# One quarter of two weight units as narrow transfers, and every load list one quarter further

## The chip, the core and the metric

The kernel runs on one core of a Trainium2 chip: TensorE (PE, with PEld for its weight loads), VectorE (DVE), ScalarE (ACT), GpSimd (POOL), SyncE (SP), on-chip memory of 128 partitions, and 16 DMA engines that carry out the transfers which the engines issue into queues. The metric is the device time of one execution in microseconds. Before the change it is 435.75 us, the median of three runs (435.31 to 435.78).

## What is computed

Causal attention with a bias that only lowers scores, for 8 batches and 8 heads of 576 tokens by 64, then a mixing of the sequence in its spectrum: the first 64 modes of the real Fourier transform along the tokens are each multiplied by a complex 512 × 512 matrix of its own, transformed back, added to the attention output and passed through one more product with a ReLU:

```python
cum = np.cumsum(np.maximum(s, 0.0), axis=-1)
bias = -(cum[:, :, :, None] - cum[:, :, None, :])
scores = np.where(causal, -1e9, q @ kT / sqrt(64) + np.minimum(bias, 0.0))
x = (softmax(scores) @ v), heads side by side            # 8 x 576 x 512
X = np.fft.rfft(x, axis=1)                                # first 64 modes used
Yr = einsum('bmd,mde->bme', Xr, w_r) - einsum('bmd,mde->bme', Xi, w_i)
Yi = einsum('bmd,mde->bme', Xr, w_i) + einsum('bmd,mde->bme', Xi, w_r)
u = x + np.fft.irfft(Y, n=576, axis=1)
out = u + np.maximum(u @ w_ch, 0.0)
```

`w_r` and `w_i` are 64 × 512 × 512 in 4-byte floats, 67.1 MB each. Reading them is most of what the kernel moves.

## The kernel before

The attention goes in N = 32 steps n. A step is a group g of two heads (four groups) and one batch b: scores, softmax, product with v, and, one step behind, the Fourier transform of that batch's 128 channels (`fft`, `fft_pick`). When the eight batches of a group are through, its part of the mode products can be taken: the matrices of the modes, 128 rows of them for each group. Those of groups 0 to 2 are done inside the later steps (`mode_products`, sums in `y_acc`), those of group 3 after the last step (`modes`, matmuls at L605 and L628), followed by the inverse transform and the product with `w_ch`.

The weights pass through five tiles `w_sb`, and at first through space in `x_all` and `y_acc` that is not yet in use. For groups 0 to 2 they are cut into 24 units u (group u // 8, sixteen modes c = u % 8 // 2, `w_r` or `w_i` by u % 2). A unit takes four loads, called quarters (`unit_loads`, L249): quarter h goes to the 32 partitions from 32h on, four modes j with 2048 values each (4 rows of 512), 512 KB as 2-byte floats in the tile, 1 MB as 4-byte floats in memory; the transfer converts. Group 3's come as 16 tiles of two loads (64 partitions each; the last is cut finer), `tile_loads` at L270.

All loads of weights, q, k and v are issued by POOL into one queue, q0, in the order in which the program gives them. Before each step a list of them is made (L727): the q and k of a coming step (`loads_qk`), its v, and as many quarters as are wanted on the chip by then, `loads_w(on_chip[n])`. `load` (L311) deals the lists evenly into one another:

```python
todo = [((i + 0.5) / len(l), x) for l in lists for i, x in enumerate(l)]
for _, (dst, src) in sorted(todo, key=lambda t: t[0]):
    nc.gpsimd.dma_start(out=dst, in_=src)
```

`on_chip[n]` counts quarters; `fits` (L326) lowers the count where a tile's former unit has not been used yet by step n. A POOL load waits for the load eight before it, and where it overwrites something for the engine that last read it: a q or k load (tile `qk`) for the transposes on PE (`tr_ps`, L454), a weight load for the mode products (`yp`, L605). `loads_w` is called again after the last step and inside `modes` (L645) for the rest of group 3.

SP has its own queue, q1. For each step from 2 on it loads the two rows of the running sums into one partition of `qt` (`cum_rows`, L441, 1 × 2 × 576 values), waiting for PE's transposes. At the end of the weights it issues `mark` (L1040), a tiny copy out of the very last weights loaded, so it waits for that load; behind it in SP's order stand the copies `yv` (L662) that spread a result over partitions, and later the outputs (L977, L981, L984).

Of the kernel before, what the change touches and what calls it, by code (L numbers as in the profile page):

```python
# [19 lines left out]
def kernel(  # L20
# [12 lines left out]
    B, H, S, D = q.shape  # L33
    NM = moe_w_r.shape[0]
    DM = H * D
    P = 128
# [189 lines left out]
    HU = WM * DM  # L226

    def slot(i, x, n=1):

        return w_sb[i][:, x * WM : (x + n) * WM, :].rearrange("p m e -> p (m e)")  # L230
# [8 lines left out]
    def parts_of(u):  # L239

        if u == 0:
            return [(0, xg[:, : 4 * HU])]
        if u == 1:
            return [(0, ya[:, HU:]), (3, xg[:, 4 * HU : 5 * HU])]
        return [(0, slot(UNIT_AT[u], 0, 4))]

    wt = {}

    def unit_loads(u):  # L249

        g, c, ri = u // NCK, u % NCK // 2, u % 2
        src = (moe_w_r, moe_w_i)[ri][:, g * P : (g + 1) * P, :]
        slots, todo = [], []
        for j0, t in parts_of(u):
            slots += [t[:, i : i + HU].rearrange("p (q e) -> p q e", q=QD) for i in range(0, t.shape[1], HU)]
        for h in range(QD):
            todo.append([])
            for j0, t in parts_of(u):
                first = 1 if ri == 1 and c + h + j0 == 0 else 0
                j1 = j0 + t.shape[1] // HU  # L260
                todo[-1].append((
                    t[QP * h : QP * h + QP, first * HU :].rearrange("p (j x) -> p j x", x=HU),
                    src[16 * c + 4 * (j0 + first) + h : 16 * c + 4 * j1 - 3 + h : 4].rearrange(
                        "j (p q) e -> p j (q e)", q=QD
                    ),
                ))
        wt[g, c, ri] = slots
        return todo

    def tile_loads(k):  # L270

        c, ri = divmod(k, 2)
        src = (moe_w_r, moe_w_i)[ri][:, (NG - 1) * P :, :]
        i, x = TILE_AT[k]
        t = slot(i, 2 * x, 2).rearrange("p (m e) -> p m e", e=DM)
        m0 = 2 * MC * (c // 2) + 2 * (c % 2)
        todo = []
        for x0, x1 in [(0, 4)] if k < NT3 - 1 else [(0, 2), (2, 4)]:
            for h in range(2):
                first = 1 if ri == 1 and c == 0 and x0 + h == 0 else 0  # L280
                todo.append((
                    t[HP * h : HP * h + HP, 2 * (x0 + first) : 2 * x1].rearrange("p (m q) e -> p m (q e)", q=2),
                    src[m0 + 4 * (x0 + first) + h : m0 + 4 * x1 - 3 + h : 4].rearrange(
                        "m (p q) e -> p m (q e)", q=2
                    ),
                ))
        wt[NG - 1, c, ri] = [t[:, :WM], t[:, WM:]]
        n = len(todo) // 2
        return [todo[:n], todo[n:]]

    NLW = 4 * NUN + 2 * NT3
    asked, queued = [0], []

    def loads_w(upto):
        todo = []
        while asked[0] < min(upto, NLW):
            if not queued:
                t = asked[0]
                queued.extend(unit_loads(t // 4) if t < 4 * NUN else tile_loads((t - 4 * NUN) // 2))
            todo += queued.pop(0)  # L300
            asked[0] += 1
        return todo

    def place_of(t):
# [21 lines left out]
    def fits(w, done):  # L326

        holds = {}
        for t in range(min(w, NLW)):
            item, end = (t // 4, t // 4 * 2 + 1) if t < 4 * NUN else (t // 2, t // 2)  # L330
            for x in place_of(t):
                if x in holds and holds[x][0] != item and holds[x][1] >= done:
                    return t
                holds[x] = item, end
        return min(w, NLW)

    on_chip = []
    for n in range(N):
        if n < B:
            w = 4 + (4 * NU + 2) * (n + 1) // (B + 1)  # L340
        else:
            w = 3 * n + 2 if n < 2 * B + 4 else max(59, 4 * n - 22)
        on_chip.append(fits(w, used[n]))


# [3 lines left out]
    first = loads_qk(0)  # L349
    load(first[:2])  # L350
    load(loads_w(2 * W0), loads_v(0) + loads_tails(0) + first[2:] + loads_v(1))
    nc.sync.dma_start(out=Ff_sb.rearrange("p T c -> p (T c)"), in_=d_Ff)
    nc.sync.dma_start(out=G_sb[:, :S], in_=d_G)
# [11 lines left out]
    with tc.tile_pool(name="cum_psum", bufs=1, space=PSUM) as cpsum:  # L365
# [29 lines left out]
        for x in range(2):  # L395
            rows = slice(NL * x, NL * x + NL)
# [222 lines left out]
    def modes(g, c, meanwhile=None, ris=(0, 1)):  # L619
# [16 lines left out]
        for x in range(2 * ris[0], 2 * ris[-1] + 2):  # L636
# [3 lines left out]
            for z in range(4):  # L640
                if meanwhile:
                    product(ri, z // 2, 2 * y + z % 2)
                else:
                    product(ri, y, z)
        load(loads_w(fits(NLW, 2 * NUN + 2 * c + ris[-1] + 1)))  # L645
        if ris[-1] == 0:
            nc.vector.tensor_tensor(out=y_acc[:, c, :], in0=ps, in1=y_acc[:, c, :], op=ALU.add)
# [68 lines left out]
    with tc.tile_pool(name="sc_psum", bufs=2, space=PSUM) as scpool, \  # L716
# [8 lines left out]
        for n in range(N):  # L725
            tails_due = loads_tails(n // B + 1)[n % B - 3 : n % B - 2] if 2 < n % B < 5 else []
            load((loads_qk(n + LA) if n % 2 else []) + (loads_vs(n) if n else loads_v(LA)) + tails_due, loads_w(on_chip[n]))  # L727
            if n == N - B:
                nc.gpsimd.dma_start(out=wch_sb, in_=moe_w_ch.rearrange("(dt p) e -> p dt e", p=P))
# [18 lines left out]
            i = first_pairs[n - N + len(first_pairs)] if n >= N - len(first_pairs) else None  # L748
# [350 lines left out]
    for step in (  # L1099
# [8 lines left out]
        i = int(step[1:].rstrip("ab"))  # L1108
# [34 lines left out]
```

## Time and profile before

The profiled execution took 435.96 us, of which the span that the profile shows is 434.2 us (mean granted TensorE clock 0.972).

| | before |
|---|---|
| median of three runs | 435.75 us |
| profiled execution / its span | 435.96 / 434.2 us |
| busy: PE, DVE, ACT, POOL | 380.6, 256.5, 249.5, 136.5 us |
| read from memory / written | 163.29 / 9.51 MB, 398 GB/s over the span |
| packets in POOL's queue q0 | 40400, 81.28 MB (as written on the chip) |
| weight loads of 512 KB: issue to landing | 17.5 us (`w_r`, 60 of them), 16.9 us (`w_i`, 55) |
| `qk` loads of 288 KB: issue to landing | 13.8 and 14.7 us (15 each) |

The page gives busy time by engine, then the span in 40 slices with the busy share in tenths for each engine and for the DMA engines, with GB/s. A group's line has what an instruction writes and reads, its count, its mean, and the idle time ahead of it with what ended that. The waits list, for each engine and line, what it waited for: total us, times, longest. The chain of work that ended last is cut short in this page at the last instructions and tells nothing of the weights, so the waits and the timeline are read in its place.

### The profile page before, as it was taken

What the parts mean: (1) busy time and instruction counts of PE and PEld (TensorE: products, weight loads), DVE (VectorE), ACT (ScalarE), POOL (GpSimd) and SP (SyncE); (2) the same over time, 40 slices, a digit from 0 to 9 for tenths busy, and PEclk for the clock granted to TensorE, in tenths of its full rate; (3) what the DMA queues carried; (4) which work ended last, traced back from release to release, by engine and by line L of the source; (5) the groups of instructions that cost most, each with busy time, mean ns of one, the idle gap of its engine ahead of it and who ended that gap; (6) DMA issues with size and microseconds to landing.
All of it is one profiled execution on the core that took longest, in us unless ns stands there. A gap on an engine that the chain in (4) does not pass through costs nothing. (4 is left out here: it accounts for less than half of the span.)

```text
span 434.2 us, 12629 instructions
## 1 busy us (share of the span) xinstructions
PE 380.6 (88%) x5395; PEld 220.2 (51%) x5395; DVE 256.5 (59%) x574; ACT 249.5 (57%) x556; POOL 136.5 (31%) x218
## 2 busy tenths in 40 slices
PE   1599999999999999999998898979879777877994
PEld 1256666546666655665665455545544334533441
DVE  7555656526775756667665565554636443671795
ACT  1387777717767765666775356545542343451894
POOL 6463333131333223233322222222222222210582
PEclk9999999989999999999999699998989998999998
DMA  8999999999999999999999999999999999995798
GB/s 157 210 207 210 214 207 209 213 214 210 210 211 211 207 212 214 212 211 208 211 212 212 212 212 211 213 212 214 212 210 212 211 211 211 211 211 103 224 365 316
DMA packets 47105, 92.87 MB, mean 214 GB/s; under 512 B 8222, under 2 KB 17946, under 8 KB 47050
## 3 DMA queue, kind: packets, MB, share of 16 engines
q0 software_dynamic: 40400, 81.28, 99.5%
q1 hardware_dynamic: 6650, 10.80, 7.4%
q8 instruction: 42, 0.69, 0.6%
q14 instruction: 13, 0.11, 0.1%
HBM read 163.29 MB, written 9.51 MB: 398 GB/s over the span
## 5 line engine op out<-in xcount | busy, mean ns | idle before, releaser
L513 ACT ACTIVATE p_sb<-sc_ps,cumt_sb 128x320 f16<-128x320 f32 (+1 forms) x384 | 161.1, 519 | 37.6 <-PE sc_ps L504 37.6
L504 PE MATMUL sc_ps<-qt,kt 128*64 128x256 bf16 (+3 forms) x640 | 95.9, 295 | 2.3 <-ACT kt L458 1.7
L504 PEld LDWEIGHTS <-kt 128*128 128x128 bf16 (+1 forms) x640 | 50.5, 126 | 62.7 <-issue 36.0
L315 POOL DMA_DIRECT2D w_sb<-in_moe_w_i_dram x62 | 35.2, 568 | 88.0 <-DMA w_sb<-in_moe_w_r_dram 32.0
L458 DVE COPY qt<-tr_ps 64x576 bf16<-64x576 bf16 x64 | 47.7, 745 | 18.3 <-PE tr_ps L454 18.0
L550 DVE RECIPROCAL rcp<-av_ps 128x5 f32<-128x5 f32 x64 | 12.4, 194 | 77.9 <-PE av_ps L545 77.9
L315 POOL DMA_DIRECT2D w_sb<-in_moe_w_r_dram x60 | 34.0, 567 | 77.5 <-DMA w_sb<-in_moe_w_r_dram 24.3
L493 PE MATMUL sc_ps<-negm,ident 128*128 128x512 bf16 x128 | 51.0, 399 | 0.0
L545 PEld LDWEIGHTS <-p_sb 128*128 128x128 f16 x1088 | 40.7, 98 | 3.6
L454 PE MATMUL tr_ps<-ident,qk 64*64 64x64 bf16 x1152 | 31.6, 198 | 10.7 <-DVE kt L458 5.2
L475 ACT ACTIVATE p<-sc_ps,cumt 128x64 f16<-128x64 f32 x32 | 10.1, 314 | 53.3 <-PE sc_ps L471 53.3
L458 ACT COPY kt<-tr_ps 64x576 bf16<-64x576 bf16 x32 | 22.9, 716 | 23.7 <-DVE qt L458 23.2
L454 PEld LDWEIGHTS <-qk 64*64 64x64 bf16 x1152 | 24.3, 112 | 23.2 <-DVE kt L458 8.3
L496 PE MATMUL sc_ps<-negm,ident 128*128 128x256 bf16 x128 | 35.9, 281 | 0.0
L545 PE MATMUL av_ps<-va,p_sb 128*128 128x65 f16 x768 | 35.0, 194 | 0.0
L605 PE MATMUL yp<-w_sb,xs 64*32 64x512 bf16 (+1 forms) x704 | 30.9, 414 | 4.3 <-DMA w_sb<-in_moe_w_i_dram 2.3
L551 DVE TENSOR_TENSOR x_all<-av_ps,rcp 128x320 f16<-128x320 f32 x64 | 31.5, 492 | 2.2
L617 DVE TENSOR_TENSOR y_acc<-yp,y_acc 128x512 f32<-128x512 f32 x34 | 21.9, 687 | 14.9 <-PE yp L605 14.9
L545 PE MATMUL av_ps<-vb,p_sb 128*128 128x65 f16 x320 | 26.0, 195 | 0.0
L315 POOL DMA_DIRECT2D vr<-in_v_dram x22 | 15.1, 687 | 31.1 <-DMA w_sb<-in_moe_w_r_dram 8.8
L458 DVE COPY kt<-tr_ps 64x576 bf16<-64x576 bf16 x32 | 24.4, 763 | 0.4
L684 ACT COPY w_sb<-z_ps 128x512 f32<-128x512 f32 x20 | 11.7, 587 | 22.5 <-PE z_ps L703 16.1
(127 smaller groups left out, 539.3 us busy)
## 6 DMA issues: line engine op xcount, KB each, us to landing
w_sb<-in_moe_w_r_dram POOLq DMA_DIRECT2D x60, 512.0 KB, 17.5
w_sb<-in_moe_w_i_dram POOLq DMA_DIRECT2D x55, 512.0 KB, 16.9
out_dram<-w_sb SPq DMA_DIRECT2D x16, 512.0 KB
qk<-in_q_dram POOLq DMA_DIRECT2D x15, 288.0 KB, 13.8
qk<-in_k_dram POOLq DMA_DIRECT2D x15, 288.0 KB, 14.7
vr<-in_v_dram POOLq DMA_DIRECT2D x14, 256.0 KB, 15.5
x_all<-in_moe_w_r_dram POOLq DMA_DIRECT2D x4, 512.0 KB, 9.9
y_acc<-in_moe_w_i_dram POOLq DMA_DIRECT2D x3, 384.0 KB, 7.1
```

Of the source, the lines that this page charges most:

```text
L315: nc.gpsimd.dma_start(out=dst, in_=src)
L454: nc.tensor.transpose(ps[rows, r, :], src[rows, r, :], ident16[rows, rows])
L458: copy(out=to[:, :, :, half * RH : half * RH + RH], in_=ps[HP * i : HP * i + HP].rearrange("d r (h p) -> d h p r", h=2),)
L493: nc.tensor.matmul(ps[:, : 2 * W], ident16, both, start=True, stop=False, skip_group_check=True)
L496: nc.tensor.matmul(ps[:, S : S + W], ident16, negm[:, NMB + m0 : NMB + m0 + W], start=True, stop=False, skip_group_check=True,)
L504: nc.tensor.matmul(ps[rows, c0 : c0 + i1 - i0], keys, qh[:, i0:i1], start=False, stop=True, skip_group_check=True,)
L513: nc.scalar.activation(out=pt[:, o : o + n_], in_=ps[:, c0 : c0 + n_], func=ACTF.Exp, bias=cumt_sb[:, x, pidx : pidx + 1], scale=0.125,)
L545: nc.tensor.matmul(ps[:, I, :NCH], lhsT, rhs, start=(i == 0), stop=(i == len(todo) - 1), skip_group_check=True,)
L550: nc.vector.reciprocal(out=rcp, in_=ps[:, :, D])
L551: nc.vector.tensor_tensor(out=x_all[:, g, b, :, D * h : D * h + D], in0=ps[:, :, :D], in1=rcp.unsqueeze(2).to_broadcast([P, NT, D]), op=AL ...
L605: nc.tensor.matmul(ps[hp][32 * j : 32 * j + 32, :], cols[k0:k1, q_, c0 : c0 + 4 * B, 4 * c + j], wt[g, c, ri][j][k0:k1, q_, :], start=(ri ...
L617: nc.vector.tensor_tensor(out=y, in0=ps[hp], in1=y, op=ALU.add)
```

## The change

There are two edits. In units 7 and 12, quarter 1 (partitions 32 to 63) no longer goes as one transfer. Its place in the order keeps a transfer of 16 partitions (32 to 47). The other 16 partitions follow as four transfers of eight partitions: partitions 48 to 55 whole (8 × 4 × 2048 values); then of partitions 56 to 63 the first 128 values of modes 0 and 1 (8 × 2 × 128), the other 1920 values of all four modes (8 × 4 × 1920), and the first 128 values of modes 2 and 3. Each is put into the list when the count of quarters asked for has reached 4u + 2 plus the number in `BEHIND`, so that other quarters lie between, and, as the lists are dealt into one another, q, k and v loads too. POOL issues 207 loads in place of 199; the bytes are the same.

The second edit raises `on_chip` by one quarter (512 KB on the chip, 1 MB read) from step 8 on. `fits` lowers the raised count only at step 31, to 102, which is the count before the change too.

```diff
+    BEHIND = {7: (1, 3, 5, 9), 12: (1, 3, 5, 7)}
+    pieces = []
     wt = {}
 
     def unit_loads(u):
...
         wt[g, c, ri] = slots
+        if u in BEHIND:
+            (dst, src), = todo[1]
+            todo[1] = [(dst[:16], src[:16])]
+            for i, after in enumerate(BEHIND[u]):
+                rows = slice(24, 32) if i else slice(16, 24)
+                x = slice(0, HU) if i == 0 else slice(P, HU) if i == 2 else slice(0, P)
+                j = (slice(0, 4), slice(0, 2), slice(0, 4), slice(2, 4))[i]
+                pieces.append((4 * u + 2 + after, (dst[rows, j, x], src[rows, j, x])))
         return todo
...
             todo += queued.pop(0)
             asked[0] += 1
+            while pieces and pieces[0][0] == asked[0]:
+                todo.append(pieces.pop(0)[1])
         return todo
...
         if n < B:
             w = 4 + (4 * NU + 2) * (n + 1) // (B + 1)
         else:
-            w = 3 * n + 2 if n < 2 * B + 4 else max(59, 4 * n - 22)
+            w = 3 * n + 3 if n < 2 * B + 4 else max(60, 4 * n - 21)
         on_chip.append(fits(w, used[n]))
```

The order of POOL's loads round unit 7 (numbers are partitions) is then: the 32 partitions of its quarter 0; a v load; the 16 partitions; quarter 2; eight partitions whole; a v load; quarter 3; the first quarter of unit 8; the first tiny piece; a quarter; q; a quarter; k; the piece of 8 × 4 × 1920; v; three quarters with a v load among them; the second tiny piece; the next q and k.

## Prediction

> **What bounds the kernel now.** I read four views: the page's slices and queues, the waits, the timeline round the last load, and windows by stage.
>
> The page (40 slices of 10.9 us; queues with packets, MB and share of sixteen DMA engines' time):
>
> ```profile
> DMA  8999999999999999999999999999999999995798
> GB/s 157 210 207 210 214 207 209 213 214 210 210 211 211 207 212 214 212 211 208 211 212 212 212 212 211 213 212 214 212 210 212 211 211 211 211 211 103 224 365 316
> ...
> q0 software_dynamic: 40400, 81.28, 99.5%
> ...
> q8 instruction: 42, 0.69, 0.6%
> q14 instruction: 13, 0.11, 0.1%
> ```
>
> The transfers run at one rate, some 211 GB/s, until slice 36. q0 holds POOL's loads, four fifths of which are weights. Two small queues, q8 and q14, fetch instructions on the same engines; they matter below.
>
> The waits (what waits for what: us in total, times, longest), POOL's, then SP's, then PE's:
>
> ```profile
> POOL w_sb L315 <- DMA w_sb<-in_moe_w_r_dram: 56.4, 32, 2.5
> POOL w_sb L315 <- DMA w_sb<-in_moe_w_i_dram: 42.9, 24, 2.6
> POOL qk L315 <- PE tr_ps L454: 27.3, 7, 7.9
> ...
> SPq L1040 <- DMA w_sb<-in_moe_w_i_dram: 64.1, 1, 64.1
> ...
> PE tr_ps L454 <- DMA qk<-in_k_dram: 3.4, 2, 2.1
> ```
>
> POOL issues a load when the eighth before it has landed, so about eight are under way and POOL waits for the transfers, not they for it. Its longest other wait is 7.9 us for PE.
>
> The timeline at the last weight load (start, length):
>
> ```profile
> 399.21 0.65 PE L628 MATMUL yp<-w_sb,xs 128*32 128x512 bf16 x4 [0.41 <-DMA w_sb<-in_moe_w_i_dram]
> 399.22 0.26 SPq L1040 DMA_DIRECT2D mark<-w_sb  x1
> 399.53 0.63 SPq L662 DMA_DIRECT2D yv<-y_sb  x1
> ```
>
> The last load lands at 399.17 us; 35.0 us of tail follow to the end at 434.2. Loads of the tail (no weights) don't change, so the time moves one for one with that landing. 434.2 + 1.8 us around it make the profiled run's 435.96, 0.2 above the median 435.75; I subtract from both alike.
>
> Windows by stage (us; PE, PEld, DVE, ACT, POOL busy; clock; DMA share; GB/s):
>
> ```profile
> 36.00:228.00 192.00, 187.53 (x3195) 115.29 (x3194) 121.67 (x292) 130.89 (x309) 57.43 (x97) 0.99 1.12 211
> ...
> 312.00:396.00 84.00, 67.75 (x688) 36.59 (x688) 39.81 (x69) 31.75 (x60) 18.24 (x30) 0.96 1.10 207
> ```
>
> PE is 98% busy early, but idle 16.2 us in the 84 before the end: what delays PE early is made up there, unless it delays POOL's loads.
>
> **The sixteen engines don't end together.** The trace has each engine's completion of each load. For the last weight load they spread over 391.80 to 399.17 us. Behind the last one stand, in us: 0, 0.45, 1.27, 1.43, 1.44, 1.46, 1.80, 1.90, then 2.57, then 4.21, 5.03, 5.86, 6.00, 6.64, 6.87, 7.36. At 18 us the spread was 1.4 us. Two things drive it apart. Each 16 KB packet of q8 holds one engine 0.95 us and makes the next three packets slower, 1.1 us in all; 42 packets over eight engines are 5 or 6 each, 5.6 to 6.7 us: these are the eight latest ("the fetching eight"). The packet durations show the fetches coming round with period eight. The two-row loads of `qt` (30 of them, L441) put a 1152-byte packet and a completion on two engines, some 0.06 us each, 1.8 us in all; followed through the completions, these two belong to the other eight. One of them, called b here, also took about four half-microsecond steps that coincide with q14's 8 KB packets (13 in all) and is the ninth late one, 2.57 us behind the last.
>
> **The change part by part.** *Narrow transfers.* From the packet records an engine starts its next packet after 305 ns for 4096 bytes, 154 for 2048, 79 for 1024, 41 for 512: 0.074 ns per byte, so 286 for 3840 bytes and 22 for 256. A completion adds 8 ns. A whole quarter is 8 packets of 4096 bytes on each engine: 8 × 305 + 8 = 2.45 us. In its place: the 16-partition transfer, 4 packets on each of sixteen, 1.23 us; eight rows of 4 × 4096, on eight engines 1.23 us; eight rows of 4 × 3840, 1.15; two tiny ones, 2 × 22 + 8 = 0.05 each. Neither "eight engines" nor which eight is shown in this trace. Few-row loads here do stay on few engines (two for `qt`). If successive narrow transfers take turns between two groups of eight, the order big, tiny, big, tiny puts both big ones on the same eight:
>
> loaded eight: 1.23 + 1.23 + 1.15 + 0.02 = 3.63 instead of 2.45: +1.18 a unit, +2.36 for two (0.02 for completions posted by all);
> relieved eight: 1.23 + 0.05 + 0.05 + 0.02 = 1.35 instead of 2.45: −1.10, −2.20 for two.
>
> *Which eight.* Few-row transfers begin at some first engines; `qt`'s two lie outside the fetching eight. That is the only row that bears on it, and I take it: the first group of eight is the one without fetches, and the fetching eight are relieved. New lateness against today's last: fetching eight 0 − 2.20; b −2.57 + 2.36 = −0.21; the next −4.21 + 2.36 = −1.85. Engine b is the new last: **−0.2 us**. Nine tenths of the fetching eight's gain are lost to one engine. Bounds: −2.2 if b is spared, +2.36 if the loaded eight are the fetching ones.
>
> [...]
>
> *Port price of few partitions.* No load into 8 partitions is in the trace. Nearest rows: the `yv` spreads into 16 partitions, 128 packets of 1024 bytes in 0.71 to 0.76 us, 172 to 185 GB/s against the stream's 215 (16 × 4096 bytes in 305 ns), and slower ones (1.2 to 1.7 us) beside outputs. Bounds: 0 and a factor 215/182 = 1.18 on the 7.2 us that the loaded engines spend in narrow ones, +1.3 us. Between these I take 0: b trails the next of the loaded engines by 0.9 to 1.2 us (at 110 us 2.5 against 1.3; at 180 us at least 2.8 against 1.9), so it works on its narrow piece, 1.2 us long, when its neighbours have nearly left theirs. [...]
>
> *Eight more issues on POOL* (207 instead of 199), 0.56 us each: 4.5 us, hidden in its 56.4 + 42.9 us of waits for weights. What would remove the cover is an engine running dry. From the completions, at every issue after 20 us even the fastest engine has at least 3.4 us queued; eight under way now include tiny ones, and replaying the stream with the new sizes leaves at least 3.3 us. If it were gone, each dry spell would cost up to an issue, 0.6 us.
>
> *One quarter more from step 8 on.* Bytes and their number stay; the order changes: `qk` and `vr` loads stand behind one more quarter, at most 2.45 us later. What is late next is PE's transposes (L454). Spare of `qk` tiles before use: 1.2 to 1.5 us at steps 18 and 22, 5.9 at 24, none at 26 and 30 (the 3.4 us above). So PE may lose up to 2.45 us at some four steps; 10 at the most, against the 16.2 idle. POOL waits for tr_ps too (the 27.3 us), and with it every load behind; the slowest of these left 4.8 us of queued transfers, 2.35 after a 2.45 us delay. SP's `qt` loads (L441) wait on the same transposes, and no weight waits for SP. I take 0; bounds 0 and +2.45 (one such cover gone wholly). Nothing here makes the landing earlier: engines never stop, so asking earlier buys nothing.
>
> Sum: −0.2 + 0 + 0 + 0 = −0.2 us; 435.75 − 0.2 is 435.55, given as **435.5**.
>
> **Rivals.** (A measurement here can tell about 0.2%, 0.87 us.)
>
> 1. *The loaded eight are the fetching eight* (the other side): +2.36 on the last engine, **438.1**. For: nothing shows which group begins. Against: `qt`'s engines. It decides as soon as the latest fetching engine gets more than 0.87 us extra. A mixed group (narrow transfers not beginning at a boundary) gives +0.5 to +2.4.
>
> 2. *b is spared.* The half-microsecond q14 steps of b need not fall on b again once the program differs: 13 packets over eight engines are 1.6 each, b has four. With the mean b ends 1.2 us earlier, new last −1.4: **434.3**; at best −2.2, the fetching eight: 433.5. Decides from 0.7 us less on b. For: only four events make b late. Against: the same loop issues the same instructions, so they may well fall alike.
>
> 3. *Narrow pieces are slowed* by their few partitions: −0.2 + 1.3 = **436.9**, more if neighbours run abreast. For: 172 to 185 against 215 GB/s. Against: b's distance.
>
> 4. *PE late, then POOL late*: **436.8 to 438.2** (+1 to +2.45). For: `qk` with no spare at two steps. Against: 16.2 us idle, 2.35 us cover.
>
> 5. *The eight-row transfers spread over all sixteen*: no shift, four more completions a unit cost 8 × 8 ns = 0.06 us: **435.8**. The change would not do what it is shaped for.
>
> **How the numbers follow.** Likeliest 0.38 (own range 434.9 to 436.4: −0.8 for b's q14 steps, +0.9 for ports or PE in part); rival 1 0.17; rival 2 0.27; rival 3 0.08; rival 4 0.06; rival 5 0.04. Faster: rival 2, 0.27. Same: likeliest and rival 5, 0.42. Slower: 1, 3 and 4, 0.31. The range reaches into rival 2 as far as −1.65 (434.1) and past rival 1's 438.1 to 438.3; left out are the best of rival 2 (0.1) and the worst of 3 and 4 and a mixed sum (0.1).
>
> **What the changed kernel's profile will show.** Right: the eight-row pieces' data packets on eight engines; the spread of the last weight load's completions shrinks from 7.4 to about 5 us, with one engine last and the fetching eight 2 us behind it; L1040's issue stands 35.0 us before the end, at 399.0. Rival 1: the spread grows to about 12 us and L1040 to 401.6. Rival 2: L1040 at 397 to 398, b among the rest. Rival 3: packets of the narrow pieces longer than 305 ns. Rival 4: longer waits of PE for `qk` and of POOL for tr_ps, and idle transfers in the slices. Rival 5: sixteen engines with data for each piece. q8 still has about 42 packets. The prediction is wrong above all if lateness isn't additive engine by engine, or if other small queues fall elsewhere.

## The result and the profile after

The changed kernel takes 440.38 us, the median of six runs (439.08 to 443.13), against 436.01 us for the kernel before in the same comparison: 1.0109 times as long by the comparison of the runs, 95% interval 1.0081 to 1.0137 (the medians alone give 1.0100). Ratios and intervals below are of the same kind, each against the kernel before in its own comparison. The forecast was 435.5 us with a range up to 438.3. The profiled execution has a span of 438.9 us, 4.7 more than before.

The slices and queues of the changed kernel's page (40 slices, now of 11.0 us each):

```profile
DMA  8999999999999999999999999999999999996598
GB/s 160 208 209 210 212 210 207 214 214 211 208 210 209 209 213 207 191 205 201 156 209 214 213 210 212 212 212 213 215 211 211 212 212 210 211 212 126 196 366 324
...
q0 software_dynamic: 40784, 81.28, 99.2%
...
q8 instruction: 42, 0.69, 0.6%
q14 instruction: 13, 0.11, 0.1%
```

Bytes and instruction fetches are those of before; of the 384 packets more, 64 have 256 bytes (the tiny pieces) and 320 have 4 bytes; eight more loads with sixteen completions each make 128 of these, and what the other 192 are for the records do not show. The rate is what changed: 191, 205, 201 and 156 GB/s in the slices from 175 to 219 us, where before no slice from the second to the 36th lay under 207. That is where unit 12 is loaded.

Windows by stage, the same stretches in both kernels (PE, PEld, DVE, ACT, POOL busy; clock; DMA share; GB/s). Before:

```profile
100.00:122.00 22.00, 21.81 (x364) 13.37 (x362) 15.77 (x38) 15.46 (x37) 6.75 (x12) 1.00 1.12 211
170.00:186.00 16.00, 15.85 (x294) 9.85 (x294) 10.80 (x26) 11.91 (x28) 4.86 (x9) 1.00 1.10 211
206.00:212.00 6.00, 5.92 (x114) 3.96 (x113) 3.81 (x12) 4.99 (x12) 2.16 (x4) 1.00 1.13 208
```

After:

```profile
100.00:122.00 22.00, 21.81 (x373) 13.67 (x372) 14.89 (x36) 16.33 (x39) 6.98 (x12) 1.00 1.12 209
170.00:186.00 16.00, 15.85 (x273) 9.47 (x273) 11.41 (x26) 9.39 (x22) 4.38 (x8) 1.00 1.14 193
206.00:212.00 6.00, 6.00 (x82) 3.05 (x79) 4.16 (x11) 3.41 (x8) 1.31 (x3) 0.68 0.77 121
```

Where unit 7 is loaded (100 to 122 us) little is lost, 209 GB/s against 211. Round unit 12 two different things happen. From 170 to 186 us the DMA engines are busier than before (1.14 against 1.10) and move less (193 against 211): their packets take longer. What the 4096-byte packets that start there last beyond 324 ns, the median, adds up to 22.2 us against 0.4 before. From 206 to 212 they are partly idle (0.77 against 1.13). Why the same pieces cost so much less round unit 7 was not found.

The waits of PE between 80 and 230 us explain the second:

```profile
PE yp L617 <- DMA w_sb<-in_moe_w_r_dram: 6.7, 2, 6.3
PE yp L617 <- DMA w_sb<-in_moe_w_i_dram: 2.3, 2, 1.9
```

Before, PE had no wait for weights in that time. L617 is the mode product (L605 before). The timeline of PE, and then of POOL:

```profile
203.66 1.93 PE L617 MATMUL yp<-w_sb,xs 64*32 64x512 bf16 x28 [6.27 <-DMA w_sb<-in_moe_w_r_dram]
```

```profile
210.69 0.59 POOL L327 DMA_DIRECT2D qk<-in_q_dram  x1 [6.40 <-PE tr_ps L466]
```

By the completion records the last tiny piece of unit 12 landed at 203.62 us. It had been put behind the 57th quarter, which step 18 asks for, and step 20 multiplies with unit 12. PE stood 6.3 us, its granted clock was 0.50 from 200 to 206 us, and POOL's next q load waited 6.4 us for PE's transposes; with eight loads under way at 203.59 us and nothing new until 210.69, when the last three of them were still landing, engines ran dry: 121 GB/s from 206 to 212 us against 208 before. At step 14 the last piece of unit 7 came 1.9 us late in the same way (141.15 us, PE at 141.19). By the start times of the steps' normalisation on DVE, step 21 stood 12.3 us later than before, step 31 only 1.9.

The end, as shown for before: the last weight load lands at 402.56 us, 3.4 later than before.

```profile
402.61 0.26 SPq L1052 DMA_DIRECT2D mark<-w_sb  x1
402.93 0.62 SPq L674 DMA_DIRECT2D yv<-y_sb  x1
```

PE's product with these weights:

```profile
404.45 0.65 PE L640 MATMUL yp<-w_sb,xs 128*32 128x512 bf16 x4
```

From there to the end it is 36.3 us in place of 35.0. PE starts it only at 404.45, 1.9 us after the landing and with no idle time ahead of it, where before it followed the landing by 0.04 us. So 3.4 of the 4.7 us are transfers and 1.3 are PE behind.

The sixteen completions of that load now stand, behind the last, between 0 and 3.44 us, against 7.36 before. The narrower spread isn't the gain that was forecast: in the dry spell at 206 to 212 us the early engines had nothing to do until new loads came, the earliest from 207.14 us on. That this is what closed the spread was not tried.

### The profile page after: what moved, and what is told of

It is laid out like the page before. It is cut to its first block, busy times and chain, and to the rows that moved or that the text cites. A ratio compares the mean times of both kernels' runs of the same rounds, so it can differ in the third digit from the quotient of the medians.

```text
span 438.9 us, 12639 instructions
## 1 busy us (share of the span) xinstructions
PE 381.5 (87%) x5395; PEld 220.5 (50%) x5395; DVE 256.6 (58%) x574; ACT 248.9 (57%) x556; POOL 140.6 (32%) x226
## 5 line engine op out<-in xcount | busy, mean ns | idle before, releaser
L327 POOL DMA_DIRECT2D w_sb<-in_moe_w_i_dram x66 | 37.5, 569 | 91.4 <-DMA w_sb<-in_moe_w_r_dram 29.6
L327 POOL DMA_DIRECT2D w_sb<-in_moe_w_r_dram x64 | 36.1, 564 | 86.5 <-DMA w_sb<-in_moe_w_r_dram 31.5
L617 PE MATMUL yp<-w_sb,xs 64*32 64x512 bf16 (+1 forms) x704 | 31.1, 409 | 10.9 <-DMA w_sb<-in_moe_w_r_dram 6.7
L617 PEld LDWEIGHTS <-xs 64*32 64x32 bf16 (+1 forms) x768 | 16.4, 139 | 21.4 <-issue 16.3
```

What stands on the lines that cost most here:

```text
L617: nc.tensor.matmul(ps[hp][32 * j : 32 * j + 32, :], cols[k0:k1, q_, c0 : c0 + 4 * B, 4 * c + j], wt[g, c, ri][j][k0:k1, q_, :], start=(ri ...
```

## The experiments

Two theories were set against each other at first, and a third came from the first results. **L**: the last pieces are late for PE. **E**: eight engines carry more, among them late ones. **N**: packets that go into few neighbouring partitions get in each other's way. N came out of the packet records: the 4096-byte packets that start between 90 and 230 us last 324 ns in the median, and what they last beyond that adds up to 6.6 us before and 38.0 us after, the longest 534 ns and 1168 ns. This sum is called *lengthening* below. Lengthening, landings and completions come from one profiled execution of each kernel; times and ratios come from all its runs.

**The second edit alone.**

```diff
-            w = 3 * n + 2 if n < 2 * B + 4 else max(59, 4 * n - 22)
+            w = 3 * n + 3 if n < 2 * B + 4 else max(60, 4 * n - 21)
```

> Only the second edit: every list from step 8 on asks one quarter more; all quarters go whole. Theory L (late pieces: the changed kernel loses because PE reaches the mode products of units 7 and 12, steps 14 and 20, before their last narrow piece has landed, 1.9 and 6.3 us, and POOL's q load then waits for PE): no such wait here, time of before within 0.3%. Theory E (eight engines: the narrow pieces load engines that were already late by 2.4 us): also no change. A loss of 1 us or more here would say that the second edit itself costs, through later q and k loads.

Measured: 0.9997 (0.9975 to 1.0019). Lengthening 9.4 us, last landing 399.35. One quarter more alone costs nothing, as forecast; the loss comes with the narrow transfers.

**The first edit alone.**

```diff
-            w = 3 * n + 3 if n < 2 * B + 4 else max(60, 4 * n - 21)
+            w = 3 * n + 2 if n < 2 * B + 4 else max(59, 4 * n - 22)
```

(against the changed kernel)

> Only the first edit: the narrow pieces, with the old counts in the lists. Counts 39 and 57, at which the last pieces go out, are then reached one step later (13 and 19 in place of 12 and 18). Theory L: PE waits longer at steps 14 and 20, by up to a step (8 us) each; time 443 to 450 us. Theory E: the engines carry the same bytes as in the full change: +2.4 us to +4.4 us over before, 438.4 to 440.4.

Measured: 1.0202 (1.0156 to 1.0248), median 444.42. Lengthening 48.6 us, last landing 405.39; PE's waits for weights between 80 and 230 us are 5.0 us and 2.5 us at the longest, about those of the changed kernel (6.3 and 1.9), and not longer by up to a step, as L had it. The time itself lies in the range that L gave (443 to 450 us) and not in E's, but the waits that were to make it do not. So the second edit takes away about half of what the first one costs, and the time moves without longer waits of PE for weights.

**The pieces early.**

```diff
-    BEHIND = {7: (1, 3, 5, 9), 12: (1, 3, 5, 7)}
+    BEHIND = {7: (1, 2, 3, 4), 12: (1, 2, 3, 4)}
```

> Both edits, the narrow pieces of units 7 and 12 at 1, 2, 3 and 4 behind the second quarter in place of 1, 3, 5, 9 and 1, 3, 5, 7: all of a unit is asked for a step or more earlier; the same shapes in the same order. Theory L: the waits of PE for weights at steps 14 and 20 go, and the time is that of before plus what the uneven engines make of it, -1 to +0.5 us. Theory E: the uneven load stays, +2.4 us (438.4) or the whole +4.4.

Measured: 1.0148 (1.0094 to 1.0203). PE's waits for weights between 80 and 230 us shrank to one:

```profile
PE yp L617 <- DMA w_sb<-in_moe_w_i_dram: 0.8, 1, 0.8
```

The kernel is no faster for it. L alone is refuted. Lengthening is 66.6 us, the largest of all; the 3840-byte packets of unit 7, 305 ns in the changed kernel, took up to 744 ns. Windows (100 to 128 and 170 to 206 us):

```profile
100.00:128.00 28.00, 27.73 (x490) 17.35 (x487) 19.84 (x48) 20.44 (x49) 8.24 (x14) 1.00 1.16 192
170.00:206.00 36.00, 34.61 (x576) 20.75 (x576) 23.91 (x54) 21.41 (x50) 11.83 (x20) 0.91 1.12 202
```

From 100 to 128 us the share is 1.16 and the rate 192, against 1.13 and 209 in the changed kernel: where the narrow transfers stand closer together, packets last longer and less is moved.

**A late piece without narrow transfers.**

```diff
         if u in BEHIND:
             (dst, src), = todo[1]
-            todo[1] = [(dst[:16], src[:16])]
...
+            todo[1] = [(dst[:, :, P:], src[:, :, P:])]
+            pieces.append((4 * u + 2 + BEHIND[u][3], (dst[:, :, :P], src[:, :, :P])))
```

> Both edits, but no narrow transfer: quarter 1 of units 7 and 12 goes as 32 partitions by 4 x 1920 at its place, and its first 128 values of each mode as a 32 x 4 x 128 transfer where the changed kernel has its last piece. The sixteen engines carry equal shares. Theory L: PE's waits at steps 14 and 20 stay, shortened by what the slowest engine is earlier (1 to 4 us at step 20), and of the +4.4 us at least half. Theory E: no loss, the time of before within 0.5 us.

Measured: 1.0005 (0.9983 to 1.0026). Lengthening 4.5 us. PE's wait is there all the same:

```profile
PE yp L613 <- DMA w_sb<-in_moe_w_r_dram: 4.4, 1, 4.4
```

Step 20 came 6.3 us later than before and step 31 0.5 us earlier. By the ten runs a PE wait of this size costs nothing that can be told from the noise: PE makes it up, or most of it, while it would wait for weights anyway. This is the other half of the case against L. The profiled execution does show a remainder: its last load lands at 398.95 us, but PE starts the product with it only at 401.27, and from the landing to the end it is 36.8 us in place of 35.0.

**Other partitions, otherwise the changed kernel.**

```diff
-            todo[1] = [(dst[:16], src[:16])]
+            todo[1] = [(dst[::2], src[::2])]
             for i, after in enumerate(BEHIND[u]):
-                rows = slice(24, 32) if i else slice(16, 24)
+                rows = slice(3, 32, 4) if i else slice(1, 32, 4)
```

> The changed kernel with the same transfers in the same order, but the rows of quarter 1 dealt otherwise: the 16-partition transfer takes every second partition (32, 34 ... 62), the first eight-row piece 33, 37 ... 61 and the others 35, 39 ... 63. Theory N (neighbouring partitions: packets into few neighbouring partitions get in each other's way; in the changed kernel 4096-byte packets took 38 us more than their usual 324 ns between 90 and 230 us, 6.6 before): the lengthened packets go, below 12 us, and with them most of the loss: 435.5 to 438. Theory E (eight engines loaded unevenly, and those already late): packets don't matter, the loss stays at 438.4 to 440.5. Where the truth is a sum, the lengthened packets go and some 2 us stay.

Measured: 1.0023 (1.0001 to 1.0045), median 436.71. Shapes, sizes and order are the same; only which rows a transfer takes differs. Windows:

```profile
170.00:186.00 16.00, 15.86 (x280) 9.78 (x274) 11.42 (x26) 10.41 (x25) 4.89 (x8) 1.00 1.11 212
...
206.00:212.00 6.00, 6.00 (x80) 3.83 (x80) 2.19 (x5) 3.69 (x10) 4.03 (x7) 0.68 0.86 132
```

Lengthening is 6.8 us, as before the change, and 170 to 186 us are back at 212 GB/s. Some 0.86 of the 1.09%, 3.7 of 4.8 us, was the price of neighbouring partitions; with the noise of the two comparisons, 2.2 to 5.3 us. PE still waits at step 20:

```profile
PE yp L617 <- DMA w_sb<-in_moe_w_r_dram: 5.1, 1, 5.1
```

The dry spell at 206 us is still there too, with the last landing at 400.13.

One thing neither this run nor the later ones take apart. A partition's row on the chip and its row in memory (8 KB for each mode) belong together, so a transfer over every second or fourth partition also reads every second or fourth 8 KB. Whether the packets of neighbours get in each other's way at the partitions or in memory was not tried; "the price of neighbouring partitions" stands for both.

**Other partitions and early.**

```diff
-    BEHIND = {7: (1, 3, 5, 9), 12: (1, 3, 5, 7)}
+    BEHIND = {7: (1, 2, 3, 4), 12: (1, 2, 3, 4)}
```

(against the kernel of the run before this one)

> The same dealing of rows with the pieces at 1, 2, 3 and 4 behind, as in the run with early pieces, which lost 1.5% and had 67 us of lengthened 4096-byte packets. Theory N: 435.5 to 438, lengthened packets below 12 us. Theory E: about 441, as with neighbouring rows.

Measured: 1.0056 (1.0026 to 1.0085), median 438.50, the ten runs from 436.60 to 441.20. Lengthening is 20.0 us in place of 66.6, so not all gone: the limit of 12 was missed, the time is just above the range too, and why packets are still lengthened was not found. The profiled execution is the shortest of the ten, 436.60 us (span 434.8, last landing at 400.08), so this landing is earlier than that of a usual run.

**Sixteen partitions, all engines alike.** Every quarter of units 7 and 12 as two transfers of 16 partitions, neighbours in one kernel, every second partition in the other (that the sixteen engines share them alike, four packets of 4096 bytes each, is the author's estimate):

```diff
         if u in BEHIND:
-            (dst, src), = todo[1]
...
+            todo = [[(dst[r], src[r]) for (dst, src) in l for r in (slice(0, 16), slice(16, 32))] for l in todo]
```

> No eight-row piece at all: all four quarters of units 7 and 12 go as two transfers of 16 neighbouring partitions, one behind the other at the quarter's place, all sixteen engines loaded alike; the second edit stays. Eight quarters are 19.6 us of the stream. [...] Theory E: no loss beyond 8 more issues, 435.5 to 436.5.

(against the kernel with neighbours)

```diff
-            todo = [[(dst[r], src[r]) for (dst, src) in l for r in (slice(0, 16), slice(16, 32))] for l in todo]
+            todo = [[(dst[r], src[r]) for (dst, src) in l for r in (slice(0, 32, 2), slice(1, 32, 2))] for l in todo]
```

> The same two transfers of 16 partitions for each quarter of units 7 and 12, but every second partition in the one and the others in the second. Theory N: packets at their usual length and the time of before, 435.5 to 436.5; the difference to the run with neighbouring partitions is then the price of the neighbours alone. If 16-partition transfers cost for another reason (their number, their source rows), this run is as slow as that one.

Measured: neighbours 1.0076 (1.0046 to 1.0106), every second 1.0022 (1.0000 to 1.0043). Lengthening 59.2 us against 8.4. Windows of the first and of the second kernel:

```profile
100.00:122.00 22.00, 21.82 (x377) 13.58 (x370) 16.14 (x38) 15.31 (x36) 7.98 (x14) 1.00 1.21 191
170.00:186.00 16.00, 15.90 (x275) 9.84 (x268) 10.46 (x25) 10.84 (x26) 5.89 (x10) 1.00 1.11 192
```

```profile
100.00:122.00 22.00, 21.82 (x373) 13.64 (x370) 14.98 (x37) 16.29 (x39) 8.72 (x15) 1.00 1.12 210
170.00:186.00 16.00, 15.92 (x255) 9.48 (x255) 9.72 (x24) 10.56 (x25) 6.54 (x11) 0.91 1.10 211
```

The same number of transfers of the same bytes: 191 and 192 GB/s for neighbours, 210 and 211 without. The difference is 0.54% or 2.4 us on 19.6 us of stream; the two kernels differ in nothing but which rows a transfer takes. The last landings, 401.98 and 399.67 us, differ by as much. The 2.4 us are 12% of that stream, with the noise of the two comparisons 4 to 20%, so the yv rows' 18% is not ruled out; that the whole stream slowed as its longest packets did is: these took up to 708 ns, 2.2 times the usual 324.

**Half way.** The 16-partition transfer as in the change, the eight-row pieces over every second partition of 48 to 63:

```diff
-                rows = slice(24, 32) if i else slice(16, 24)
+                rows = slice(17, 32, 2) if i else slice(16, 32, 2)
```

> The changed kernel with its 16 neighbouring partitions (32 to 47) as they are; the eight-row pieces take every second partition of 48 to 63 (48, 50 ... 62 and 49, 51 ... 63) in place of 48 to 55 and 56 to 63. Theory N, as a matter of how many neighbours: between the changed kernel (38 us of lengthened 4096-byte packets, +1.1%) and every fourth partition (6.8 us, +0.2%); if the eight-row pieces make the price, 15 us or less and about 437 us; if the 16-partition transfers make it, 30 us or more and about 440.

Measured: 1.0039 (1.0020 to 1.0059), lengthening 17.0 us. So it goes 38.0, 17.0 and 6.8 us for eight-row pieces over eight neighbours, over 16 partitions and over 32 (the last with the 16-partition one spread as well). The eight-row pieces among eight neighbours are the larger part of the price.

**Which eight engines.** Every fourth partition, early, tiny pieces first (against the run with other partitions and early):

```diff
-                rows = slice(3, 32, 4) if i else slice(1, 32, 4)
-                x = slice(0, HU) if i == 0 else slice(P, HU) if i == 2 else slice(0, P)
-                j = (slice(0, 4), slice(0, 2), slice(0, 4), slice(2, 4))[i]
+                rows = slice(1, 32, 4) if i == 3 else slice(3, 32, 4)
+                x = slice(0, HU) if i == 3 else slice(P, HU) if i == 1 else slice(0, P)
+                j = (slice(0, 2), slice(0, 4), slice(2, 4), slice(0, 4))[i]
```

> The early pieces with every fourth partition, in the order tiny, large, tiny, large in place of large, tiny, large, tiny, so that by turn-taking the other eight engines carry the large ones. Before, the last weight load landed at 399.17 us, with large first at 400.08. If the large ones had all gone to the engines without instruction fetches (as the prediction took it), they go to the fetching eight here: 401.5, 2.4 over before. If they had gone to the fetching eight, the other way round: 399.0. If the two groups of eight cut through the fetching ones, it stays between: 399.6 to 401, and about 1 us over before again.

Measured: 1.0071 (1.0043 to 1.0100), last landing 401.92. The completions of the last weight load, us behind the fastest engine, for the kernel before, large first and tiny first:

```
before       0 0.49 0.72 1.36 1.50 2.33 3.15 4.79 5.46 5.56 5.90 5.92 5.93 6.09 6.91 7.36
large first  0 0.52 2.21 2.54 3.19 3.24 3.29 3.49 3.58 3.95 4.22 4.74 5.16 6.07 6.92 6.99
tiny first   0 0.28 0.70 1.01 1.53 2.12 2.64 3.03 3.80 3.81 8.12 8.80 8.94 9.14 9.16 9.32
```

With tiny first six engines stand apart, over 8 us behind the fastest, and the weights land 2.75 us later than before (1.84 later than with large first), near the 401.5 expected if the fetching eight carry the large pieces. That the order decides which engines are loaded rests on these two executions alone: in time the two orders can't be told apart, 1.0056 (1.0026 to 1.0085) against 1.0071 (1.0043 to 1.0100). I read the lists as two groups that cut through the fetching eight, two of them loaded with large first and six with tiny first; that split is inferred, not seen engine by engine.

**Two engines further on, or back.** The 128-value pieces are cut so that a piece of two partitions (or of six) goes ahead of the first large one:

```diff
+            eight, few, rest = slice(3, 32, 4), slice(3, 8, 4), slice(11, 32, 4)
...
+                (1, few, slice(3, 4), slice(0, P)),
+                (1, slice(1, 32, 4), slice(0, 4), slice(0, HU)),
+                (2, eight, slice(0, 1), slice(0, P)),
+                (3, eight, slice(0, 4), slice(P, HU)),
+                (4, eight, slice(1, 2), slice(0, P)),
+                (4, rest, slice(3, 4), slice(0, P)),
+                (4, eight, slice(2, 3), slice(0, P)),
```

> The early pieces with every fourth partition, large first, and the 128-value pieces cut otherwise: a two-partition piece goes ahead of the first large one and a six-partition piece behind, so that, if narrow transfers take turns over the sixteen engines one after another, the large ones begin two engines further on. With tiny first, six engines ended 8.1 to 9.3 us behind the fastest and apart from the rest: so six of the fetching eight carried the large ones there, and two of them in the changed kernel's order. If turn-taking goes engine by engine, a shift by two in one direction relieves all eight fetching engines and in the other loads four of them. Relieved: the last weight load lands at 399.0 (by the prediction's sum), the spread is about 5 us. Otherwise: four engines stand late and apart, landing 400.5 to 401.5. If engines are not taken in turn, as in the early run, 400.1.

In the other run `rest` goes first, then tiny, large, tiny, large, and `few` at the end.

> The same with the six-partition piece ahead and the order tiny, large, tiny, large, by which the large ones begin two engines further back. Relieved or four late, the other way round than in the run shifted up; the better of the two lands at 399.0 and takes 435.6 us, within 0.2% of before.

Measured: 0.9993 (0.9972 to 1.0013) and 1.0003 (0.9980 to 1.0026); last landings 399.44 and 399.08, spreads 5.77 and 5.35 us. By landing and spread both are relieved, neither has four engines apart. The expectation that exactly one would be was wrong, so the rule by which engines are taken stays open. Both spread less than before (7.36) and land within 0.3 us of before, as the prediction's sum for a relieved group says (399.0); neither beats the kernel before. Lengthening is 15.0 and 14.4 us here, hardly less than the 17.0 us of the run half way, which took 0.39% longer than before: the sum tells neighbours from spread rows when it is large, and does not turn into time one for one.

## Why the prediction was wrong

*What bounds the kernel, and the tail.* Right. In the runs whose last landing was later, the end moved with it: landings at 401.98 (halves), 404.03 (early pieces) and 405.39 us (first edit alone) gave spans of 437.1, 438.8 and 440.5, tails of 35.1, 34.8 and 35.1 us. Two executions have a longer tail: the changed kernel's, 36.3 us, and that with the late piece and no narrow transfers, 36.8 us.

*Price of few partitions.* This is the step that failed. The prediction said "Between these I take 0", and gave +1.3 us as the upper end. The runs show 3.7 us, the difference between 1.0109 and 1.0023. Two things were wrong in it. The reason for the 0 was that engine b arrives when its neighbours have left; but the records show 161 lengthened packets among 5240 of 4096 bytes (over 1.3 times the median), 33 among 5516 before, so the price doesn't hang on one engine's distance. And the nearest row, `yv` into 16 partitions at 172 to 185 GB/s, is no bound for eight: with eight rows among neighbours single packets lasted up to 1168 ns, where none of before lasted over 534 in the same 90 to 230 us. How the partitions lie is what counted: lengthening goes 38.0, 17.0 and 6.8 us as they are spread. With 16 neighbours single packets took up to 708 ns against 324, but the time grew by only 2.4 us on 19.6 us of stream. The spread of the engines over several us may be why so few packets meet; no run shows it, nor why neighbours get in each other's way; the ports that the prediction names in its heading and its range are in no trace of this case, longer packets are. The prediction took 0; the 3.7 us measured lie above its upper end of 1.3. As rival 3 the slower narrow pieces were named, at 436.9 us and with a chance of 0.08; the price was too small by a factor of nearly three.

*Which eight.* That a piece of eight partitions keeps to eight engines, which the trace of before did not show, can be read from the changed kernel's packets: the 32 of 3840 bytes of each unit start in eight rows of four, 284 to 286 ns apart within a row. Which eight is not shown either way. The prediction took it that the fetching eight are all relieved, with one engine left, −0.2 us. With every fourth partition, early pieces landed the weights at 400.08, 0.9 later than before and in the range of the mixed group (+0.5 to +2.4), a case that shared the 0.17 of rival 1; that is one execution, the fastest of its ten. The sum engine by engine is not refuted: if the tiny-first order loads late engines (401.92) and the shifted ones spare them (399.08 to 399.44), the landings fit it. But no record here names an engine, that few-row transfers begin at some first engines was the author's assumption, and the shifted runs did not come out as counting by it said.

*One quarter more.* Right taken alone: 0.9997. But the step asked only who waits for q and k. That PE needs the last piece of units 7 and 12 at steps 14 and 20 was not looked up, and there it waited 1.9 and 6.3 us. The cover named for PE, its idle time before the end, took up nearly all of this: the run with the late piece alone shows 1.0005. In the changed kernel PE was 12.3 us late at step 21 and at the end still behind the weights: the 1.3 us of tail. Why it was behind there stays open: PE was 10.4 us late at step 21 with every fourth partition too, and that tail is 35.0 us. One thing that sets apart the two executions with a longer tail is the granted clock between 379 and 400 us: 0.84 in the changed kernel and 0.76 with the late piece, against 1.00 before and 0.92 with every fourth partition. That the clock is the reason was not tried.

*Eight more issues on POOL.* Not seen as a cost: the two shifted kernels issue 213 loads, 14 more than before, and take the time of before. But "at least 3.3 us" of queued work was too high. In the changed kernel, the work still queued on the fastest engine at an issue fell to 2.0 us at 187 us and to nothing at 210.69.

The sum of the changed kernel, in its own profile: 4.7 us, of which 3.4 stand in the last landing and 1.3 in PE. Of the 1.09% between the kernels, some 4.8 us, 3.7 go with neighbouring partitions; what is left, 0.23% or 1.0 us (0.01 to 0.45%), holds the uneven engines and the late pieces together.

## What to carry to other kernels

Where a transfer is cut into fewer partitions, ask which partitions, not only how many: taking every second or every fourth one removed 0.86 of the 1.09% here, at no change of shape or order. Read the DMA share beside GB/s: here a share that rose while the rate fell (1.14 at 193 GB/s) went with longer packets, and a share that fell (0.77 at 121) with missing issues. When a load is put off, look up the step that consumes it, and then whether the waiting engine has idle time later to make it up.

## What was not expected of the hardware

Packets of 4096 bytes that lasted 324 ns in the median lasted up to 1168 ns in the changed kernel. Bunches of about twice the median go with neighbours: 607 to 649 ns at 178 us here, 607 to 708 ns at 174 us with 16 neighbouring partitions. Single long packets stand without neighbours too: with every fourth partition and early pieces a few lasted up to 1304 ns (large first) and 1647 ns (tiny first), and no reason was found. Transfers that are themselves wide pay too: the 2304-byte packets of q and k (192 ns in the median) between 90 and 205 us lasted 10.8 us beyond that in all, against 0.8 before, the longest 414 ns. Still longer ones, up to 813 ns, stand at 212 us, when the loads start again after the dry spell and no narrow transfer is under way; with the late piece and no narrow transfers at all some reached 1025 ns at 206 us.

In the one execution of each that was profiled, the last landing depends on the order of the narrow transfers (400.08 us with large first, 401.92 with tiny first), but pieces of two and of six partitions did not shift it as counting engine by engine would have.
